# Attention kernel in one slot loop: the output projection as pairs of 64-row matmuls in two banks, and one maxima task moved by two groups

## The chip, the cores and the metric

The kernel runs on one core of one Trainium2 chip. The metric is the device time of one execution in microseconds. TensorE (PE) multiplies matrices into PSUM; ScalarE (ACT), VectorE (DVE) and GpSimd (POOL) do the rest, the first two from PSUM too; SyncE's queue (SP) issues most DMAs.

## What is computed

Two attention blocks over the same 2048 rows of 512 numbers, with 32 heads of 16, are mixed by a gate. All is in float32.

```python
def _A_ref(x, wq, wk, wv, wo, beta):     # 4 segments of 512 rows
    logits = jnp.einsum("bhqd,bhkd->bhqk", qs, ks) * scale + mask     # causal in the segment
    p = _softmax(logits, axis=-1)
    a_dot = jnp.einsum("bhqk,bhkd->bhqd", p, vs)
    a_mem = num / den                    # what the segments before left in M and z
    o = g * a_mem + (1.0 - g) * a_dot
    return o @ wo

def _B_ref(x, wqkv, wo):                 # all 2048 rows, no mask
    p = _softmax(jnp.einsum("bhqd,bhkd->bhqk", q, k) * (Dh ** -0.5), axis=-1)
    return (p @ v) @ wo

g = _sigmoid((x * gate_w).sum(-1, keepdims=True))
return g * _A_ref(...) + (1 - g) * _B_ref(...)
```

The weights of A are so large that its softmax needs exact row maxima. Products that must be exact are made from two halves of each number, a high and a low one, with three of the four terms (TERMS).

## The kernel before

After a first part (projections, memory of A) comes a loop of 32 **slots** `k`. A slot handles one unit of A and one of B; a unit is four heads by 512 queries. It has 37 **groups** `n`: 32 of B, then 5 of A. The program is written out in order and nothing reorders it: each engine works through its instructions as the Python code emits them.

In a group of B, TensorE does three things:

- the **score pair** (`t_group`, line 537): two matmuls with 64 rows of contraction, one on rows 0 to 63 and one on rows 64 to 127 of the array, into two banks of PSUM. ScalarE takes the exponential of each bank into `raw` (line 543);
- the **maxima pair** (`s_b`, line 474), a task for the next slot's unit: two 64-row matmuls into the two banks of a *score pair* buffer `sbk`; VectorE takes the maximum of both banks in one instruction (line 476). In groups 0 to 31 there is one such task, put between the two matmuls of the score pair (`mid`);
- the **products** with the values (`pv`, line 559) of an earlier group, into `pvb`.

PSUM has eight banks: `tb0`, `tb1` and `mb` for scores and anything else (`misc()` and the score pairs take the one used longest ago), `pvb`, and two buffers `sbk0` and `sbk1` of two banks each, which the maxima tasks use in turn (`rot("s", SBK)`). A matmul into a bank waits until the last reader of it is done.

In slots 9 to 30, group 1 also holds a call of the **output projection** for 128 rows of the segment before (`out_mm`, line 625): twelve matmuls with all 128 rows of contraction into one `misc()` bank. A call with `a == 0` does A's half, and ScalarE copies the bank to `yo` (line 629); the next slot's, with `a == 1`, does B's, VectorE adds the bank to `yo` (line 632), and SyncE's queue stores it. The operands `oh` and `ol` are made at the end of every second slot (`out_split`, line 618 on ScalarE and 619 on GpSimd). In group 0 the products of the slot before are finished and VectorE copies them out (`fin_copy`, line 566); SyncE's queue stores that copy and later loads parts of it back (`fin_load`, 576 and 578), and VectorE works on these from group 13 on (`fin_rec`, line 583).

Slot 0 has four groups (0, 2, 4, 6) with an own job of the first part (`fill`) and a second maxima task; both tasks stand between the two matmuls of the score pair there.

Of the kernel before, what the change touches and what calls it, by code (L numbers as in the profile page):

```python
# [7 lines left out]
FT = mybir.dt.float32  # L8
# [3 lines left out]
AF = mybir.ActivationFunctionType  # L12
OP = mybir.AluOpType
# [7 lines left out]
DM = 512  # L21
C = 512
NC4 = SEQ // C
NT = SEQ // 128
# [10 lines left out]
def gated_mix_kernel(ctx, tc, xt, wq, wk, wv, wo, beta, wqkv, wob, gate_w, out):  # L35
    nc = tc.nc
    outr = out.rearrange("b s d -> (b s) d")
# [47 lines left out]
    SBK = [PS.tile([128, 2, C], FT, name=f"sbk{i}") for i in range(2)]  # L85
    lru = []

    def bank(allowed):
        b = min(allowed, key=lambda a: max([n for n, x in enumerate(lru) if x is a], default=-1))
        lru[:] = [x for x in lru if x is not b] + [b]  # L90
        return b
# [3 lines left out]
    def misc():  # L95
        return bank(mode["misc"])
# [12 lines left out]
    def rot(key, lst):  # L109
        i = cnt.get(key, 0)  # L110
        cnt[key] = i + 1
        return lst[i % len(lst)]
# [165 lines left out]
    TERMS = ((0, 0), (0, 1), (1, 0))  # L278
# [127 lines left out]
    def load_q(u):  # L406
        kd, qd, c = UN[u]
        load_qk(q_of(u), kd, 0, qd, c)

    def load_ka(u):  # L410
        kd, qd, c = UN[u]
        load_qk(KA[u % 2], kd, 1, qd, c)

    def load_kb(k, c=None):
        dst = KB[k % 3] if c is None else KB[k % 3][:, :, c * C:(c + 1) * C]
        load_qk(dst, "B", 1, k % 8, c)
# [6 lines left out]
    def load_vb(g):  # L423
        v_src(VB[g % 2], "B", g % 4, None)

    def load_va(u):
        kd, qd, c = UN[u]
        v_src(VA[(u // 2) % 2], "A", qd // 2, c)
# [89 lines left out]
    AT = {}  # L518
# [102 lines left out]
    def out_mm(c, t, a):  # L621
# [8 lines left out]
        else:  # L630
            tt = 4 * c + t
            nc.vector.tensor_tensor(AT["yo"], b, AT["yo"], op=OP.add)
            nc.sync.dma_start(outr[tt * 128:(tt + 1) * 128, :], AT["yo"])

    def tail_ops(t):
        s = KB[2 * (t // 2)][:, t % 2]
        return [s[:, 1024 * n:1024 * n + 1024].rearrange("p (g a t) -> p g a t", g=4, a=2) for n in range(2)]
# [29 lines left out]
    def todo(fn, *a):  # L667
        return lambda: fn(*a)
# [90 lines left out]
    for blk in range(16):  # L759
        g, c = divmod(blk, 4)  # L760
# [8 lines left out]
        n = blk + 1 + (c == 2)  # L769
# [92 lines left out]
    def pvs(k, n):  # L862

        ua, ub = k, 32 + k
        if n == 0:
            if k:
                pv(ua - 1, 2)
                fin_copy(ua - 1)
        elif k == 31 and n < 2 * NT:
            if n % 2 and n > 1:  # L870
                pv(ub, n // 2 - 1)
        elif 2 <= n < 2 * NT + 2:
            pv(ub, n // 2 - 1, n % 2 * 256, n % 2 * 256 + 256)
            if n == 2 * NT + 1:
                fin_copy(ub)
        elif n > 2 * NT + 1:
            m = n - 2 * NT - 2
            if m < 2:
                pv(ua, 0, 256 * m, 256 * m + 256)
            else:  # L880
                pv(ua, 1)
                pv(ua, 3)

    def extras(k):

        pre, post = {}, {}
        if not k:
            for n in range(4):
                pre[2 * n] = [fill[n - 4]]
        post[2 * S_LAST + 4] = [todo(m_rows, k + 1)]  # L890
        for n, at in [(k - 9, 1)] + [(23, 2 * OMI)] * (k == 31):
            if n >= 0:
                pre[at] = [todo(out_mm, n // 8, n // 2 % 4, n % 2)]
        return pre, post

    def beside(k, it):
# [26 lines left out]


    ex = [extras(k) for k in range(32)]
    plan = {}

# [4 lines left out]
    for k in range(31):  # L932
# [5 lines left out]
        for n, t in enumerate(ST_A):  # L938
            plan.setdefault((k, 2 * NT + n - (n > 2)), []).append(todo(s_a, k + 1, *t))

    for k in range(32):
        ua, ub = k, 32 + k
        banks = T3 + [b[:, 0] for b in SBK] * (k == 31)
        for n in range(NG):
            it = n // 2 if n < NG - 1 else NT + 2
            mid = plan.pop((k, n)) if n < 2 * NT and (k, n) in plan else []
            t_group(*(ub, n) if n < 2 * NT else (ua, n - 2 * NT), banks, mid)
            for f in plan.get((k, n), []) + ex[k][0].get(n, []):
                f()
            pvs(k, n)  # L950
            for f in ex[k][1].get(n, []):
                f()
            if n % 2 == 0 and n < NG - 1:
                continue
            beside(k, it)
            if it == S_LAST:
                m_chain(k + 1)
            if it == 4 and not k:
                late()
            if it == 4 and not k:  # L960
                load_q(ub + 2)
                for c in range(NC4):
                    load_kb(2, c)
            if it == NT and k < 29:
                load_q(ub + 3)
                load_kb(k + 3)
            if it == 6 and k < 31:
                load_q(ua + 1)
                load_ka(ua + 1)
                if (ua + 1) % 2 == 0:  # L970
                    load_va(ua + 1)
            if it == 9:
                if k % 2 == 0 and k < 30:
                    load_vb(k // 2 + 1)
                if 1 <= k <= 4:
                    load_wo(k - 1)
# [55 lines left out]
```

## Time and profile before

| what | us |
|---|---|
| median of the runs | 1946.82 |
| fastest run | 1943.4 |
| the profiled execution | 1946.74 |
| its span | 1945.0 |
| TensorE busy in it | 1922.5 |
| VectorE busy | 1622.1 |
| ScalarE busy | 1434.8 |
| GpSimd busy | 298.4 |

A matmul's bar in the profile contains its weight load and its way through the array, so bars overlap and busy time says little; what counts is the distance from start to start. In the rows, `PEld` is the weight loads, a tile name like `tb<-qb,xh` is what is written and what is read, and `x4` is four instructions of one kind merged. TensorE's clock was granted in full in the whole span.

### The profile page before, as it was taken

The numbers are of one execution on the slowest core, as the hardware profiler recorded it, in microseconds if no ns is written. First come the engines' busy times: TensorE is split into PE (matmuls) and PEld (weight loads), VectorE is DVE, ScalarE is ACT, GpSimd is POOL, SyncE is SP. The second block draws the span as 40 slices with busy tenths as digits, with TensorE's granted clock in tenths as the row PEclk, the third lists the DMA queues.
The fourth block names the chain that finished last, engine by engine and source line by source line (L and its number), as shares of the span: only waits on it lengthen the run. The fifth ranks groups of instructions, "written<-read, shape, count | busy, mean of one in ns | idle before, by whom it ended". The sixth has DMA issues, their size and how long they took to land.

```text
span 1945.0 us, 43560 instructions
## 1 busy us (share of the span) xinstructions
PE 1922.5 (99%) x17485; PEld 931.0 (48%) x17485; DVE 1622.1 (83%) x1726; ACT 1434.8 (74%) x2699; POOL 298.4 (15%) x593
## 2 busy tenths in 40 slices
PE   7999999999999999999999999999999999999999
PEld 5887777444344444444444444444444444444445
DVE  6135766899999999999999999999999999999942
ACT  4233333688888888888888888888888888888884
POOL 5200000011111111111111111111111111111022
PEclk9999999999999999999999999999999999999999
DMA  7666656745444444443445454544444443434111
GB/s 217 163 207 185 196 193 173 176 96 116 98 117 88 105 87 105 87 116 87 116 87 114 87 115 87 116 88 108 94 97 107 96 105 87 104 87 110 50 48 58
DMA packets 163790, 222.49 MB, mean 114 GB/s; under 512 B 39916, under 2 KB 90556, under 8 KB 157828
## 3 DMA queue, kind: packets, MB, share of 16 engines
q1 hardware_dynamic: 159284, 211.41, 44.1%
q0 software_dynamic: 3248, 8.03, 2.3%
q8 instruction: 138, 2.26, 0.5%
q14 instruction: 64, 0.52, 0.1%
q10 hardware_dynamic: 1056, 0.26, 0.1%
HBM read 147.95 MB, written 68.16 MB: 111 GB/s over the span
## 4 chain that ended last, share of the span: by engine, by line
PE 96%; DVE 2%; DMA 1%; SPq 1%; issue 0%; ACT 0%; DVEq 0%; ACTq 0%
PE pvb L559 33%; PE tb L537 18%; PE sbk L474 12%; PE mb L537 9%; PE tb L304 5%; PE sbk L452 3%; PE tb L625 2%; PE mb L304 2%; PE sbk L287 1%; PE tb L287 1%; PE mb L625 1%; PE pvb L304 1%; PE sbk L456 1%; PE mb L287 1%; PE pvb L287 1%; PE tb L652 1%
## 5 line engine op out<-in xcount | busy, mean ns | idle before, releaser
L476 DVE TENSOR_REDUCE mxb<-sbk 128x2 f32<-128x1024 f32 x1024 | 1225.8, 1223 | 61.0 <-PE tb L537 30.6
L543 ACT ACTIVATE raw<-tb 128x512 f32<-128x512 f32 x1555 | 887.6, 598 | 148.2 <-PE tb L537 103.6
L559 PE MATMUL pvb<-raw,vb 128*17 128x256 f32 (+1 forms) x8072 | 639.9, 388 | 0.0
L543 ACT ACTIVATE raw<-mb 128x512 f32<-128x512 f32 x782 | 467.6, 598 | 72.3 <-PE mb L537 45.7
L474 PE MATMUL sbk<-xh,qb 64*128 64x512 f32 x1344 | 477.6, 444 | 3.5 <-DVE mxb L476 2.1
L537 PE MATMUL tb<-qb,xh 64*128 64x512 f32 x872 | 353.3, 443 | 0.0
L559 PEld LDWEIGHTS pvb<-raw,vb 128*17 128x17 f32 x8072 | 135.0, 95 | 341.3 <-issue 335.9
L474 PE MATMUL sbk<-kb,qb 64*128 64x512 f32 x704 | 240.9, 444 | 0.0
L537 PEld LDWEIGHTS tb<-qb,xh 64*128 64x128 f32 x872 | 146.4, 184 | 176.6 <-issue 90.1
L537 PE MATMUL mb<-qb,xh 64*128 64x512 f32 x445 | 199.0, 447 | 0.0
L474 PEld LDWEIGHTS sbk<-xh,qb 64*128 64x128 f32 x1344 | 190.6, 184 | 8.7 <-DVE mxb L476 6.3
L537 PE MATMUL tb<-qb,kb 64*128 64x512 f32 x470 | 191.0, 446 | 0.9 <-DVE st L314 0.9
L546 POOL TENSOR_SCALAR_AFFINE_SELECT raw<-raw 128x256 f32<-128x256 f32 (+1 forms) x320 | 115.6, 361 | 357.7 <-ACT raw L543 349.9
L460 DVE TENSOR_REDUCE mx<-sbk 128x2 f32<-128x768 f32 (+1 forms) x128 | 136.7, 1090 | 23.7 <-PE sbk L456 20.9
L537 PEld LDWEIGHTS mb<-qb,xh 64*128 64x128 f32 x445 | 82.0, 184 | 94.9 <-issue 50.6
L537 PEld LDWEIGHTS tb<-qb,kb 64*128 64x128 f32 x470 | 79.2, 184 | 99.0 <-issue 53.1
L599 POOL TENSOR_TENSOR o<-o,d 128x512 f32<-128x512 f32 x31 | 39.7, 1280 | 477.7 <-DMA d<-rd 388.5
L537 PE MATMUL mb<-qb,kb 64*128 64x512 f32 x234 | 104.1, 445 | 0.0
L474 PEld LDWEIGHTS sbk<-kb,qb 64*128 64x128 f32 x704 | 96.1, 184 | 5.2 <-issue 3.4
L559 PE MATMUL pvb<-raw,va 128*17 128x256 f32 (+2 forms) x1280 | 94.7, 384 | 0.8 <-ACT pvs L568 0.8
L452 PE MATMUL sbk<-ka,qa 64*128 64x256 f32 (+3 forms) x512 | 88.0, 358 | 1.1
L311 ACT ACTIVATE st<-tb 128x512 fp32r<-128x512 f32 x33 | 19.8, 599 | 81.1 <-DVE phi L310 46.8
(288 smaller groups left out, 1864.3 us busy)
## 6 DMA issues: line engine op xcount, KB each, us to landing
xh<-dB SPq DMA_DIRECT2D x38, 512.0 KB
vb<-vdB SPq DMA_DIRECT2D x16, 1088.0 KB
dB<-st SPq DMA_DIRECT2D x64, 256.0 KB
dA<-st SPq DMA_DIRECT2D x64, 256.0 KB
pd<-pvs SPq DMA_DIRECT2D x64, 256.0 KB
kb<-dB SPq DMA_DIRECT2D x22, 512.0 KB
xh<-dB SPq DMA_DIRECT2D x38, 256.0 KB
qb<-dB SPq DMA_DIRECT2D x64, 128.0 KB
```

Of the source, the lines that this page charges most:

```text
L287: nc.tensor.matmul(b, lhs, WV[wi][:, k, :], start=n == 0, stop=n == 11)
L304: nc.tensor.matmul(b, WS[ws][w][wi][:, k, :], (XH, XL)[xi][c][:, k, :], start=n == 0, stop=n == 11)
L452: nc.tensor.matmul(b[:, j, c0:c0 + n], q_of(u)[r, p, i * 128:(i + 1) * 128], k_of(u, p)[r, :n], start=True, stop=False)
L460: nc.vector.tensor_reduce(m[:, :, p, i], b[:, :, :n], axis=AX.X, op=OP.max)
L474: nc.tensor.matmul(b[:, j], q_of(u)[r, p, i * 128:(i + 1) * 128], k_of(u, p)[r, kc * C:(kc + 1) * C], start=True, stop=True)
L476: nc.vector.tensor_reduce(MXB[u][:, :, p, i, kc], b, axis=AX.X, op=OP.max)
L537: nc.tensor.matmul(bs[j][:, c0:c0 + w], k_of(u, h // 2)[r, 128 * it:128 * it + 128], q_of(u)[r, h // 2, q0:], start=True, stop=True)
L543: nc.scalar.activation(pt, bs[j], AF.Exp, scale=SCALE)
L546: nc.gpsimd.affine_select(out=m, in_=m, pattern=[[1, 128]] if n < 2 else [[0, 2], [1, 128]], compare_op=OP.is_ge, fill=0.0, base=0, channe ...
L559: nc.tensor.matmul(PVB[32 * h:32 * h + E + 1, q0 + lo:q0 + hi], vt[:, it, 4 * q + h, :], pt[:, lo:hi], start=it == 0 and lo == 0, stop=it ...
L599: nc.gpsimd.tensor_tensor(o, o, d, op=OP.mult)
L625: nc.tensor.matmul(b, (AT["oh"], AT["ol"])[oi][:, g, a], (AT["wh"], AT["wl"])[wi][:, g, a], start=n == 0, stop=n == 11)
```

## The change

`out_rows` takes the place of `out_mm` in slots 9 to 30. It cuts the contraction of 128 rows into two of 64, rows 0 to 63 (`j == 0`) and 64 to 127 (`j == 1`). The first sums up in a `misc()` bank, the second in the first bank of an `sbk` buffer, whose turn comes with it. So a call has 24 matmuls in place of 12, and two banks to take out of PSUM. With `a == 0` ScalarE copies the one to `yo` and VectorE the other to `yp`; with `a == 1` ScalarE copies the one to `yq`, VectorE adds the other to `yp`, and GpSimd makes two additions into `yo`, which SyncE's queue then stores.

In slots 9 to 30 the maxima task of group 2 is moved to group 0, where it takes the place between the score matmuls, and group 0's own task comes behind them. In group 1 the task is no longer between the score matmuls; it stands behind the projection. Group 2 has none. In slot 0, the second task of a group that has two stands behind the second score matmul and ahead of the own job.

```diff
@@ -631,6 +631,27 @@
             tt = 4 * c + t
             nc.vector.tensor_tensor(AT["yo"], b, AT["yo"], op=OP.add)
             nc.sync.dma_start(outr[tt * 128:(tt + 1) * 128, :], AT["yo"])
+
+    def out_rows(c, t, a):
+        b = [misc(), rot("s", SBK)[:, 0]]
+        for n, (oi, wi, g) in enumerate([(oi, wi, g) for oi, wi in TERMS for g in range(4)]):
+            for j in range(2):
+                r = slice(64 * j, 64 * j + 64)
+                nc.tensor.matmul(b[j], (AT["oh"], AT["ol"])[oi][r, g, a], (AT["wh"], AT["wl"])[wi][r, g, a],
+                                 start=n == 0, stop=n == 11)
+        if a == 0:
+            AT["y"] = [AT["L"].tile([128, DM], FT, name=n) for n in ("yo", "yp")]
+            nc.scalar.activation(AT["y"][0], b[0], AF.Copy)
+            nc.vector.tensor_copy(AT["y"][1], b[1])
+        else:
+            tt = 4 * c + t
+            y0, y1 = AT["y"]
+            y2 = AT["L"].tile([128, DM], FT, name="yq")
+            nc.scalar.activation(y2, b[0], AF.Copy)
+            nc.vector.tensor_tensor(y1, b[1], y1, op=OP.add)
+            nc.gpsimd.tensor_tensor(y0, y0, y2, op=OP.add)
+            nc.gpsimd.tensor_tensor(y0, y0, y1, op=OP.add)
+            nc.sync.dma_start(outr[tt * 128:(tt + 1) * 128, :], y0)
 
     def tail_ops(t):
         s = KB[2 * (t // 2)][:, t % 2]
@@ -890,7 +911,7 @@
         post[2 * S_LAST + 4] = [todo(m_rows, k + 1)]
         for n, at in [(k - 9, 1)] + [(23, 2 * OMI)] * (k == 31):
             if n >= 0:
-                pre[at] = [todo(out_mm, n // 8, n // 2 % 4, n % 2)]
+                pre[at] = [todo(out_rows if k < 31 else out_mm, n // 8, n // 2 % 4, n % 2)]
         return pre, post
 
     def beside(k, it):
@@ -938,14 +959,17 @@
         for n, t in enumerate(ST_A):
             plan.setdefault((k, 2 * NT + n - (n > 2)), []).append(todo(s_a, k + 1, *t))
 
+    for k in range(9, 31):
+        plan[k, 0] += plan.pop((k, 2))
     for k in range(32):
         ua, ub = k, 32 + k
         banks = T3 + [b[:, 0] for b in SBK] * (k == 31)
         for n in range(NG):
             it = n // 2 if n < NG - 1 else NT + 2
-            mid = plan.pop((k, n)) if n < 2 * NT and (k, n) in plan else []
+            mid = [plan[k, n].pop()] if n < 2 * NT and (k, n) in plan and (k < 9 or n != 1) else []
             t_group(*(ub, n) if n < 2 * NT else (ua, n - 2 * NT), banks, mid)
-            for f in plan.get((k, n), []) + ex[k][0].get(n, []):
+            own, tasks = ex[k][0].get(n, []), plan.get((k, n), [])
+            for f in own + tasks if k else tasks + own:
                 f()
             pvs(k, n)
             for f in ex[k][1].get(n, []):
```

What this makes of the order, in slot 10 (a call with `a == 1`). TensorE, groups 0 and 1, before: line 537 is the score pair, 474 the maxima pair, 559 the products, 625 the projection. What a row waits for stands in brackets.

```order
L537 MATMUL tb1_111<-qb0_68,xh0_87 128x512 [waits DMAHW1_49,DMAHW0_49]
L474 MATMUL sbk0_114<-xh1_88,qb1_69 128x512 [waits DVE_49]
L474 MATMUL sbk0_114<-xh1_88,qb1_69 128x512
L537 MATMUL tb0_110<-qb0_68,xh0_87 128x512 [waits Activation_49]
L559 MATMUL pvb_112<-raw8_86,va0_76 17x256 [waits Pool_49] x2
L559 MATMUL pvb_112<-raw8_86,va0_76 17x256 x2
L537 MATMUL mb_113<-qb0_68,xh0_87 128x512
L474 MATMUL sbk1_115<-xh1_88,qb1_69 128x512 [waits DVE_49]
L474 MATMUL sbk1_115<-xh1_88,qb1_69 128x512
L537 MATMUL tb1_111<-qb0_68,xh0_87 128x512 [waits Activation_49]
L625 MATMUL tb0_110<-wh_2776,oh_2780 128x512 [waits Activation_49]
L625 MATMUL tb0_110<-wh_2776,oh_2780 128x512 x3
```

TensorE, the same place after (line 640 is the new projection):

```order
L537 MATMUL tb1_111<-qb0_68,xh0_87 128x512 [waits DMAHW1_49,DMAHW0_49]
L474 MATMUL sbk1_115<-xh1_88,qb1_69 128x512 [waits DVE_49]
L474 MATMUL sbk1_115<-xh1_88,qb1_69 128x512
L537 MATMUL tb0_110<-qb0_68,xh0_87 128x512 [waits Activation_49]
L474 MATMUL sbk0_114<-xh1_88,qb1_69 128x512 [waits DVE_49]
L474 MATMUL sbk0_114<-xh1_88,qb1_69 128x512
L559 MATMUL pvb_112<-raw8_86,va0_76 17x256 [waits Pool_49] x2
L559 MATMUL pvb_112<-raw8_86,va0_76 17x256 x2
L537 MATMUL mb_113<-qb0_68,xh0_87 128x512
L537 MATMUL tb1_111<-qb0_68,xh0_87 128x512 [waits Activation_49]
L640 MATMUL tb0_110<-wh_2776,oh_2780 128x512 [waits Activation_49]
L640 MATMUL sbk1_115<-wh_2776,oh_2780 128x512 [waits DVE_49]
```

Group 0 now has two maxima tasks, into `sbk1` and `sbk0`, and group 1 none ahead of the projection; the projection's second bank is `sbk1`, the one that group 0's first task filled, with a wait for VectorE.

TensorE behind the projection, group 2 and the start of group 3, before:

```order
L625 MATMUL tb0_110<-wl_2777,oh_2780 128x512 x4
L625 MATMUL tb0_110<-wh_2776,ol_2781 128x512 x4
L537 MATMUL mb_113<-qb0_68,xh0_87 128x512 [waits Activation_49]
L474 MATMUL sbk0_114<-xh1_88,qb1_69 128x512 [waits DVE_49]
L474 MATMUL sbk0_114<-xh1_88,qb1_69 128x512
L537 MATMUL tb1_111<-qb0_68,xh0_87 128x512 [waits Activation_49]
L559 MATMUL pvb_112<-raw8_86,vb1_2773 17x256 [waits DVE_49]
```

And after, from the projection's last matmul on:

```order
L640 MATMUL tb0_110<-wh_2776,ol_2781 128x512
L640 MATMUL sbk1_115<-wh_2776,ol_2781 128x512
L474 MATMUL sbk0_114<-xh1_88,qb1_69 128x512 [waits DVE_49]
L474 MATMUL sbk0_114<-xh1_88,qb1_69 128x512
L537 MATMUL mb_113<-qb0_68,xh0_87 128x512 [waits Activation_49]
L537 MATMUL tb1_111<-qb0_68,xh0_87 128x512 [waits Activation_49]
L559 MATMUL pvb_112<-raw8_86,vb1_2773 17x256 [waits DVE_49]
L559 MATMUL pvb_112<-raw8_86,vb1_2773 17x256 x3
```

The maxima task of group 1 follows the projection at once, then the score pair of group 2, undivided, and the products.

VectorE at the same place, before: the last maximum of A's groups (line 462), group 0's maximum, the copy of the old products and group 1's maximum stand ahead of the projection's addition (line 632).

```order
L462 TENSOR_REDUCE mx_7803<-sbk1_115 128x4 [waits PE_49]
L476 TENSOR_REDUCE mxb_7649<-sbk0_114 128x2 [waits PE_49]
L566 COPY pvs_7938<-pvb_112 128x512 [waits DMAHW1_49,DMAHW5_49,PE_49,Activation_49]
L476 TENSOR_REDUCE mxb_7649<-sbk1_115 128x2 [waits PE_49]
L632 TENSOR_TENSOR yo_7427<-tb0_110,yo_7427 128x512 [waits PE_49]
L476 TENSOR_REDUCE mxb_7649<-sbk0_114 128x2 [waits PE_49]
```

VectorE after (line 651 is the addition from `sbk1`):

```order
L462 TENSOR_REDUCE mx_7817<-sbk0_114 128x4 [waits PE_49]
L476 TENSOR_REDUCE mxb_7663<-sbk1_115 128x2 [waits PE_49]
L476 TENSOR_REDUCE mxb_7663<-sbk0_114 128x2 [waits PE_49]
L566 COPY pvs_7955<-pvb_112 128x512 [waits DMAHW1_49,DMAHW5_49,PE_49,Activation_49]
L651 TENSOR_TENSOR yp_7440<-sbk1_115,yp_7440 128x512 [waits PE_49]
L476 TENSOR_REDUCE mxb_7663<-sbk0_114 128x2 [waits PE_49]
```

Two maxima of group 0 now stand ahead of the copy, and group 1's maximum stands behind the projection's addition.

## The prediction

> **What bounds the kernel now.** I read the page first: busy times, then the chain that ended last.
>
> ```profile
> span 1945.0 us, 43560 instructions
> PE 1922.5 (99%) x17485; PEld 931.0 (48%) x17485; DVE 1622.1 (83%) x1726; ACT 1434.8 (74%) x2699; POOL 298.4 (15%) x593
> PE 96%; DVE 2%; DMA 1%; SPq 1%; issue 0%; ACT 0%; DVEq 0%; ACTq 0%
> ```
>
> TensorE is 96% of the chain, so a gain must shorten what TensorE does or waits for. The profiled execution took 1946.74 us for this span (1.74 outside it), and the median of the runs is 1946.82, so the sum below stands for both. Next the chain of waits (start, length, what): the first two and the last of the output projections that it lists among its longest pieces, twenty in the 22 slots that the change touches, all of 2.95 to 2.98.
>
> ```profile
> 786.17 2.96 PE tb L625 x12
> 835.74 2.96 PE tb L625 x12
> ...
> 1777.56 2.96 PE mb L625 x12
> ```
>
> The distance from one to the next is 49.57 us, a slot. What such a place consists of, the timeline of TensorE shows; this is slot 14, groups 0 to 3 (start, length, operation).
>
> ```profile
> 1032.02 0.50 PE L537 MATMUL tb<-qb,xh 64*128 64x512 f32 x1
> 1032.03 0.73 PE L474 MATMUL sbk<-kb,qb 64*128 64x512 f32 x2
> 1032.36 0.39 PE L537 MATMUL mb<-qb,xh 64*128 64x512 f32 x1
> 1032.69 0.63 PE L559 MATMUL pvb<-raw,va 128*17 128x256 f32 x8
> 1033.24 0.50 PE L537 MATMUL tb<-qb,xh 64*128 64x512 f32 x1
> ...
> 1033.91 1.19 PE L625 MATMUL mb<-wh,oh 128*128 128x512 f32 x4
> 1034.94 1.09 PE L625 MATMUL mb<-wl,oh 128*128 128x512 f32 x4
> 1035.87 1.07 PE L625 MATMUL mb<-wh,ol 128*128 128x512 f32 x4
> 1036.87 0.50 PE L537 MATMUL tb<-qb,xh 64*128 64x512 f32 x1
> ...
> 1037.53 0.63 PE L559 MATMUL pvb<-raw,vb 128*17 128x256 f32 x8
> 1038.08 0.50 PE L537 MATMUL mb<-qb,xh 64*128 64x512 f32 x1
> ```
>
> Two facts are to be read from the starts. Two 64-row matmuls on the two halves of the array start 0.01 us apart (1032.02 and 1032.03) and run beside each other. And every stretch of one kind costs a fixed part besides its matmuls: four projections in the middle take 1035.87 - 1034.94 = 0.93, or 0.23 each, but all twelve 2.96, which is 12 x 0.23 + 0.20. A group's two pairs take 1032.69 - 1032.02 = 0.67, again 2 x 0.23 + 0.20. Three pairs in one stretch stand in slot 0, and take 363.77 - 362.88 = 0.89, which is 3 x 0.23 + 0.20.
>
> ```profile
> 362.88 0.49 PE L537 MATMUL tb<-qb,kb 64*128 64x512 f32 x1
> 362.88 0.95 PE L474 MATMUL sbk<-xh,qb 64*128 64x512 f32 x4
> ...
> 363.77 0.63 PE L559 MATMUL pvb<-raw,vb 128*17 128x256 f32 x8
> ```
>
> About half of the 0.20 is the first weight load, which nothing covers: in group 0 the second pair's load starts 0.11 after the first's.
>
> ```profile
> 1032.02 0.18 PEld L537 LDWEIGHTS tb<-qb,xh 64*128 64x128 f32 x1 [0.21 <-issue]
> ...
> 1032.13 0.19 PEld L537 LDWEIGHTS mb<-qb,xh 64*128 64x128 f32 x1
> ```
>
> **The projection itself.** Twelve full matmuls become 24 half ones, twelve pairs. At 0.23 a pair they take what they took. What goes is the change of kind around them: before, groups 0 to 2 hold four stretches (two pairs, two pairs, twelve projections, two pairs), 4 x 0.20 + 18 x 0.23 = 4.94. After, they hold two: three pairs, then the score pair of group 1, the twelve pairs, the maxima pair and the score pair of group 2: 2 x 0.20 + 18 x 0.23 = 4.54. That is 0.40 a call, if nothing waits.
>
> **The wait that comes with it.** The second bank is half of a score pair, and the order shows that it is the half just filled by the moved maxima task. VectorE's rows of the same place:
>
> ```profile
> 1032.79 1.23 DVE L476 TENSOR_REDUCE mxb<-sbk 128x2 f32<-128x1024 f32 x1 [0.95 <-PE mb L537]
> 1033.93 0.68 DVE L566 COPY pvs<-pvb 128x512 f32<-128x512 f32 x1
> ...
> 1036.97 0.69 DVE L632 TENSOR_TENSOR yo<-mb,yo 128x512 f32<-128x512 f32 x1 [1.23 <-PE mb L625]
> 1037.63 8.53 DVE L476 TENSOR_REDUCE mxb<-sbk 128x2 f32<-128x1024 f32 x7
> ```
>
> The first is the maximum of group 0, the copy is that of the old products, the addition at 1036.97 is the projection's, and the seven maxima after it are those of groups 2 to 8. I count from the start of group 0. Its first maximum starts at 0.77 and ends at 1.99. How long TensorE takes to go on after such an end is seen where a group in slot 13 waits for one: VectorE's maximum began at 1003.24, ends 1.22 later at 1004.46, and the held maxima matmul begins at 1004.51, so 0.05.
>
> ```profile
> 1003.24 2.35 DVE L476 TENSOR_REDUCE mxb<-sbk 128x2 f32<-128x1024 f32 x2
> 1004.36 0.50 PE L537 MATMUL tb<-qb,xh 64*128 64x512 f32 x1
> 1004.51 0.58 PE L474 MATMUL sbk<-xh,qb 64*128 64x512 f32 x2
> 1004.85 0.39 PE L537 MATMUL tb<-qb,xh 64*128 64x512 f32 x1
> ```
>
> So the projection's second half may load weights at 2.04 and run from 2.15. Without a wait: group 0 takes 0.89, its products 0.56 (1033.24 - 1032.69, rounded up), so group 1 begins at 1.45, and the projection would run from 1.45 + 0.11 + 0.23 = 1.79. The wait costs 0.36. From 2.15 follow 13 steps of 0.231 (eleven more pairs, the maxima pair, the score pair), to 5.15, and 0.33 from the last pair to the products (1032.36 to 1032.69): they start at 5.48. Before, they start at 1037.53 - 1032.02 = 5.51. What is left of 0.40 is 0.03 a call, 0.7 us in 22 calls. The half that doesn't wait runs one pair ahead and meets the other at the maxima pair, whose waiting half stands first, so that lead is worth nothing. Bounds: a gain of 0.39 if the wait costs nothing, a loss of 0.1 if the release or the restart takes 0.1 longer than in the one row.
>
> The Trainium skill, "TensorEngine Tiling (Array Packing)", section "Gotcha 1: PSUM Pressure", speaks against this change: row tiling raises the pressure on PSUM, as the row tiles must write to different banks. It gives no time; the trace above gives the price of the bank that has to be borrowed.
>
> **After the projection.** VectorE gets a 0.68 copy in the 11 calls that had none; in the other 11 its addition of 0.69 stays. It has room: in a slot of 49.5 us it is busy for 46.35.
>
> ```profile
> 1033.00:1082.50 49.50, 49.46 (x508) 20.82 (x504) 46.35 (x46) 41.31 (x78) 8.37 (x17) 1.00 0.49 114
> ```
>
> (The columns are TensorE, its weight loads, VectorE, ScalarE, GpSimd, clock, DMA.) And when behind, it catches up:
>
> ```profile
> 1052.80 3.48 DVE L476 TENSOR_REDUCE mxb<-sbk 128x2 f32<-128x1024 f32 x3
> ```
>
> Three maxima in 3.48, the last of 1.22, are one per 1.13, against a group of 1.22 (1036.87 to 1038.08, with rounding). The last pair runs from 2.15 + 11 x 0.231 = 4.69 and ends 0.39 later, at 5.08; the copy starts at 5.11 and ends at 5.80, and group 3, at 5.48 + 0.55 = 6.03, wants that buffer: 0.18 to spare with the 0.05. Group 1's maximum starts 0.66 after the copy (1036.97 to 1037.63), ends at 6.99; group 4 wants its buffer at 7.25: 0.21 to spare. Cost nothing; if both margins failed, some 0.2 a call.
>
> ScalarE's second copy (11 calls) costs a place of 0.49 in its row, at an end where it has been idle for 2 us:
>
> ```profile
> 987.41 0.60 ACT L629 ACTIVATE yo<-tb 128x512 f32<-128x512 f32 x1 [2.04 <-PE tb L625]
> 987.90 0.59 ACT L543 ACTIVATE raw<-mb 128x512 f32<-128x512 f32 x1
> ```
>
> The maxima pair stands between projection and scores and gives it 0.23 + 0.23 of cover; uncovered it is part of the 0.2 above.
>
> GpSimd's two additions, 1.28 each by its group of the same shape, and the output's DMA behind them; then rows of SyncE's queue and of VectorE:
>
> ```profile
> L599 POOL TENSOR_TENSOR o<-o,d 128x512 f32<-128x512 f32 x31 | 39.7, 1280 | 477.7 <-DMA d<-rd 388.5
> ...
> 1034.64 0.34 SPq L570 DMA_DIRECT2D pd<-pvs  x1
> ...
> 1045.57 0.53 SPq L576 DMA_DIRECT2D o<-pd  x1
> ...
> 1052.37 0.24 DVE L583 RECIPROCAL rec<-rec 128x16 f32<-128x16 f32 x1
> ```
>
> The store now holds SyncE's queue until about 5.1 + 0.6 + 2.6 = 8.3, or 1040.3 here; the next entry leaves at 1045.57, so nothing is behind it. The copy of the old products comes one maximum later (1.1 us), so the load at 1045.57 may go at 1046.7; its reader is at 1052.37. Zero; uncovered, at most 1.1 in a slot.
>
> **Slot 0.** Where a group has two maxima tasks, its second score matmul no longer stands behind the second task's wait. In the chain that matmul stands with 0.23 and 0.15 at two such groups, between the late task and the next job; the group at 362.88 above has no wait.
>
> ```profile
> 352.92 0.23 PE tb L537
> ...
> 359.26 0.15 PE mb L537
> ```
>
> Four groups of slot 0 are of that kind. I take 0.5 for the slot, between 0 and 0.9.
>
> Sum: 1946.74 - 0.7 - 0.5 = 1945.5.
>
> **The rivals.** *The wait doesn't count* (15%): VectorE gives the bank back early, or TensorE gets past it. Then 22 x 0.39 + 0.5 = 9.1 us go: 1937.6. For it stands that each step of 0.20 is in the rows; against it that the held instruction stands first in an in-order queue and the maximum's 1.22 is one instruction.
>
> *VectorE's hand-over* (20%), the one that ends slower: the copy after the projection holds the borrowed bank and delays group 1's maximum, so groups 3 and 4 wait. It decides once the margins of 0.18 and 0.21 are gone, that is when projection end to release takes 0.2 more; each call then loses 0.2 to 0.3, 22 x 0.25 = 5.5: 1951. Against it: VectorE recovers 0.09 a group, and the delay in slot 13 cost only 0.15 (0.49 from its first to its last score matmul, where 1032.02 to 1032.36 is 0.34).
>
> *Loads that don't hide* (4%): in a long run of half-array pairs each load stands open, 0.11 a pair: 22 x 12 x 0.11 = 29, 1974.6. The three pairs in 0.89 speak against it. The Trainium skill, "TensorE: Matmul & The Clock Gate", section "Part 3: Packing small matmuls", lets a weight load overlap a running matmul only if the row group differs, which would make this the likely case. By that rule the full projections, all on the same rows, would be 0.23 + 0.11 = 0.34 apart; the trace has 0.23, so the measurement decides.
>
> *The halves don't overlap* (2%): 24 steps of 0.23 instead of 12, 2.76 a call, 61 us: about 2006. The starts 0.01 apart speak against it.
>
> **How the numbers follow.** 59% stay with the sum, within 3 us. The range runs from 1937, where the first rival ends, to 1952, past the second; it leaves out the last two and the edges, some 1 in 10 by these cases, as bounds from single rows are soft. Changes under 2% (39 us) are what a measurement of this kernel can hardly tell from none; only the last rival goes beyond: faster 1%, within 96%, slower 3%.
>
> **What would show it.** The new projection's weight load should wait some 0.5 us (1.56 to 2.04) for VectorE's maximum, in all 22 slots; from its first to the next products 24 + 2 + 2 matmuls should show 0.23 a pair; group 3 should begin about 6.03 after group 0, and a slot remain 49.5. I am wrong if that wait is absent, if groups 3 to 5 show waits for VectorE, or if the slot shrinks by 0.3 or more.

## The result, and the profile after

| kernel | median, us | ratio to before (95 % interval) | one slot, us |
|---|---|---|---|
| before, run beside it | 1946.02 | | 49.571 |
| after | 1943.10 | 0.9988 (0.9983 to 0.9994) | 49.529 |

The medians are over all executions; the ratios leave out two slow ones, one of before (2188.65) and one of e6_longer_wait (3425.64, at a granted clock of 0.543), and aren't the quotients of these medians.

The changed kernel takes 1.2 to 3.3 us less (the interval times 1946), which is under 2% and so no change by the bound of the prediction. The forecast was 1945.5, with a range of 1937 to 1952. The kernel before, at 1946.02, lies in that range too, so the total alone tests little; the rows below test the mechanism. The page of the kernel after, its span, its busy times and the shares of its chain:

```profile
span 1942.3 us, 44163 instructions
PE 1919.8 (99%) x17749; PEld 941.6 (48%) x17749; DVE 1624.6 (84%) x1737; ACT 1440.5 (74%) x2710; POOL 326.9 (17%) x615
PE 94%; DVE 2%; DMA 1%; SPq 1%; issue 1%; ACT 0%; DVEq 0%
```

The bound is the same: TensorE is 94% of the chain. TensorE has 264 matmuls more (17749 - 17485), twelve in each of 22 calls, and isn't busier for it.

**A slot.** Line 507 makes a transpose once in a slot, always in the same form, and so marks the slots. These rows of TensorE's timeline are those of slot 8 and slot 29; between them lie 21 slots with a call each. Before:

```profile
767.50 0.39 PE L507 MATMUL tb<-ident,m 128*32 128x128 f32 x4
...
1808.49 0.39 PE L507 MATMUL tb<-ident,m 128*32 128x128 f32 x4
```

After:

```profile
765.97 0.39 PE L507 MATMUL tb<-ident,m 128*32 128x128 f32 x4
...
1806.08 0.39 PE L507 MATMUL tb<-ident,m 128*32 128x128 f32 x4
```

So a slot took (1808.49 - 767.50) / 21 = 49.571 and now takes (1806.08 - 765.97) / 21 = 1040.11 / 21 = 49.529: 0.042 less, 0.9 us in 22 slots.

**Inside a slot.** TensorE's timeline after, slot 14 again, from group 0 (1030.28) to group 3 (1036.28). The rows left out are further rows of the same stretches.

```profile
1030.28 0.50 PE L537 MATMUL tb<-qb,xh 64*128 64x512 f32 x1
...
1031.17 0.63 PE L559 MATMUL pvb<-raw,va 128*17 128x256 f32 x8
1031.72 0.50 PE L537 MATMUL tb<-qb,xh 64*128 64x512 f32 x2
1032.06 0.39 PE L640 MATMUL mb<-wh,oh 64*128 64x512 f32 x1
...
1033.35 0.39 PE L640 MATMUL sbk<-wl,oh 64*128 64x512 f32 x1
...
1034.94 0.39 PE L640 MATMUL sbk<-wh,ol 64*128 64x512 f32 x1
1034.98 0.58 PE L474 MATMUL sbk<-kb,qb 64*128 64x512 f32 x2
...
1035.73 0.63 PE L559 MATMUL pvb<-raw,vb 128*17 128x256 f32 x8
1036.28 0.50 PE L537 MATMUL mb<-qb,xh 64*128 64x512 f32 x1
```

The weight loads at the start of the projection, same kernel and slot. In brackets stand the idle time before a row and what ended it.

```profile
1031.95 0.18 PEld L640 LDWEIGHTS mb<-wh,oh 64*128 64x128 f32 x1
...
1032.33 0.18 PEld L640 LDWEIGHTS sbk<-wh,oh 64*128 64x128 f32 x1 [0.19 <-DVE mxb L476]
```

And VectorE's timeline there: the two maxima of group 0, the copy of the old products, the projection's addition, and the maxima that follow.

```profile
1031.05 2.36 DVE L476 TENSOR_REDUCE mxb<-sbk 128x2 f32<-128x1024 f32 x2 [0.94 <-PE sbk L474]
1033.32 0.68 DVE L566 COPY pvs<-pvb 128x512 f32<-128x512 f32 x1
...
1035.37 0.69 DVE L651 TENSOR_TENSOR yp<-sbk,yp 128x512 f32<-128x512 f32 x1 [1.37 <-PE sbk L474]
1035.98 4.74 DVE L476 TENSOR_REDUCE mxb<-sbk 128x2 f32<-128x1024 f32 x4
```

Counted from the start of group 0, at 1030.28:

| event | predicted | after |
|---|---|---|
| first half of the projection runs | 1.79 | 1.78 |
| second half's weight load | 2.04 | 2.05 |
| one pair | 0.231 | 0.227 (1.59 / 7, from 1033.35 to 1034.94) |
| VectorE's addition starts | 5.11 | 5.09 |
| products of group 2 | 5.48 | 5.45 |
| next maximum | 5.77 | 5.70 |
| group 3 | 6.03 | 6.00 |

Group 3's score matmuls start at 1036.28 and 1036.62 and its maxima pair at 1036.29, the 0.34 of a group without a wait, so VectorE gave the buffer back in time.

**The waits.** The view of waits of the kernel after, its three groups of weight loads at line 640 (us in all, times, longest one):

```profile
PEld sbk L640 <- DVE mxb L476: 2.1, 11, 0.2
...
PEld tb L640 <- ACT raw L543: 1.8, 7, 0.3
...
PEld mb L640 <- ACT raw L543: 1.0, 4, 0.3
```

Only half of the 22 calls show VectorE, with 0.19 each. The other eleven are the calls with `a == 0`. There the end of a segment's `out_split` (a row of 1.06 on ScalarE ahead of group 0's exponentials) makes the exponentials late, and the projection's *first* bank is held back by ScalarE, to about 1.88. The second half still waits for VectorE until 2.04, but no longer long enough to be a row of its own: idle time counts from the end of the load before. In slot 14, too, the second half's load is 0.38 behind the first's (1032.33 - 1031.95), and only 0.19 of it is idle in this view, since the load before ended at 1031.95 + 0.18 = 1032.13.

In slot 14 ScalarE is close behind as well. Its exponential of the projection's first bank:

```profile
1031.31 0.59 ACT L543 ACTIVATE raw<-mb 128x512 f32<-128x512 f32 x1
```

It ends at 1031.90, and the first half's load goes at 1031.95, which is 1.67 after group 0. That costs nothing here, since the matmul (1.78) stands behind the score pair anyhow.

**Slot 0.** The two profiled spans differ by 1945.0 - 1942.3 = 2.7, but 0.9 of it lies in the 22 slots. A part of the rest isn't the change. These are windows of 3.41 us in slot 0 (window; length; then busy time of TensorE, its weight loads, VectorE, ScalarE, GpSimd; granted clock; DMA share; GB/s). Before:

```profile
345.48:348.89 3.41, 3.41 (x9) 2.63 (x9) 1.34 (x2) 0.49 (x1) 0.00 (x0) 0.50 0.73 241
```

After:

```profile
345.48:348.89 3.41, 3.41 (x23) 1.97 (x21) 1.48 (x2) 0.66 (x2) 1.28 (x2) 1.00 0.75 225
```

In the chain of before the job that stands there is this step (start, length):

```profile
345.34 4.56 PE mb L304 x12
```

And in the chain of after:

```profile
344.84 2.99 PE mb L304 x12
```

The profiled execution of before ran these matmuls at half the clock for 3.41 us, which cost 4.56 - 2.99 = 1.57. (The sentence ahead of the prediction, that the clock was granted in full in the whole span, misses this stretch.) It isn't a property of the one kernel or the other, as the second experiment shows. A second stretch at about half the clock, which the sentence misses too, lies between 52 and 59 us in both profiles (0.52 before, 0.53 after), and so makes no difference between them. So the time of the change is better read from the slots and from the ratio of the runs than from two spans.

### The profile page after: what moved, and what is told of

Its sections match the earlier page's. It is cut to its first block, busy times and chain, and to the rows that moved or that the text cites. A ratio compares the mean times of both kernels' runs of the same rounds, so it can differ in the third digit from the quotient of the medians.

```text
span 1942.3 us, 44163 instructions
## 1 busy us (share of the span) xinstructions
PE 1919.8 (99%) x17749; PEld 941.6 (48%) x17749; DVE 1624.6 (84%) x1737; ACT 1440.5 (74%) x2710; POOL 326.9 (17%) x615
## 4 chain that ended last, share of the span: by engine, by line
PE 94%; DVE 2%; DMA 1%; SPq 1%; issue 1%; ACT 0%; DVEq 0%
PE pvb L559 33%; PE tb L537 17%; PE sbk L474 12%; PE mb L537 9%; PE tb L304 4%; PE sbk L452 3%; PE sbk L640 2%; PE mb L304 2%; PE sbk L287 1%; PE tb L287 1%; PE pvb L304 1%; PE sbk L456 1%; PE mb L287 1%; PE pvb L287 1%; DVE mxb L476 1%; PE tb L640 1%
## 5 line engine op out<-in xcount | busy, mean ns | idle before, releaser
L474 PE MATMUL sbk<-xh,qb 64*128 64x512 f32 x1344 | 467.8, 442 | 3.6 <-DVE mxb L476 2.2
L474 PE MATMUL sbk<-kb,qb 64*128 64x512 f32 x704 | 236.2, 442 | 0.2 <-DVE mxb L476 0.2
```

Source lines behind the costliest of these rows:

```text
L474: nc.tensor.matmul(b[:, j], q_of(u)[r, p, i * 128:(i + 1) * 128], k_of(u, p)[r, kc * C:(kc + 1) * C], start=True, stop=True)
```

## The experiments

The theory, W, is that of the prediction: the projection loses its fixed parts (0.40 a call), and the wait of its second half for VectorE's first maximum takes nearly all of it back. Against it stand that the gain is in slot 0 or comes from moving tasks, that the wait is hidden, and that VectorE's hand-over behind the projection is what costs. A *slot* is the distance between the rows of line 507, as above. The kernel before had a median of 1944.87 beside e1, e2, e4 and e5 and of 1946.20 beside e3, e6, e7 and e8, so go by the ratios and the slots, not by the medians of different rows.

| label | what it is | median, us | ratio to before (95 % interval) | one slot, us |
|---|---|---|---|---|
| after | all parts | 1943.10 | 0.9988 (0.9983 to 0.9994) | 49.529 |
| e1_slot0_only | slot 0's order alone | 1945.32 | 1.0004 (0.9994 to 1.0014) | 49.576 |
| e2_tasks_moved_only | all but the new projection | 1944.82 | 0.9998 (0.9987 to 1.0010) | 49.563 |
| e6_longer_wait | a bank filled later | 1970.44 | 1.0125 (1.0109 to 1.0142) | 50.678 |
| e3_task_not_moved | all but the moved task | 1962.44 | 1.0086 (1.0069 to 1.0104) | 50.390 |
| e8_pair_banks_only | both banks from one pair | 1954.17 | 1.0051 (1.0035 to 1.0068) | 50.052 |
| e4_task_in_group36 | the task one group earlier still | 1945.24 | 1.0013 (1.0001 to 1.0026) | 49.653 |
| e5_task_first_in_group0 | the task first in group 0 | 1939.73 | 0.9973 (0.9964 to 0.9982) | 49.388 |
| e7_first_and_pair_banks | e5 and e8 together | 1950.37 | 1.0028 (1.0017 to 1.0040) | 49.840 |

### One part alone: slot 0's order

The kernel after, with the old projection and the tasks where they were:

```diff
-                pre[at] = [todo(out_rows if k < 31 else out_mm, n // 8, n // 2 % 4, n % 2)]
+                pre[at] = [todo(out_mm, n // 8, n // 2 % 4, n % 2)]
...
-    for k in range(9, 31):
-        plan[k, 0] += plan.pop((k, 2))
...
-            mid = [plan[k, n].pop()] if n < 2 * NT and (k, n) in plan and (k < 9 or n != 1) else []
+            mid = [plan[k, n].pop()] if n < 2 * NT and (k, n) in plan else []
```

> The kernel before with slot 0's new order alone: the second maxima task behind the second score matmul; projection and task places as before. Theory W (the slots 9 to 30 keep only 0.04 a call, 0.9 us in all, because the wait for the borrowed bank eats 0.36 of 0.40): slot 0 gives the rest, three score matmuls of 0.23 taken out of the chain, 0.7 us, and 2.3 us in an execution in which the kernel before falls to half clock for 3.41 us there. So 1943.7 to 1945.4 with 1946.0 for before, and slots 9 to 30 at 49.57 us each as before. Rival N (the gain of the change lies in the new projection): no change here, 1946.0, and group 0 of slot 0 at its old length of 3.4 us.

The groups with two tasks are where the gain should be. TensorE's timeline before, from such a group's first score matmul to its products:

```profile
357.85 0.49 PE L537 MATMUL tb<-qb,kb 64*128 64x512 f32 x1
...
362.32 0.63 PE L559 MATMUL pvb<-raw,vb 128*17 128x256 f32 x8
```

The same group in this kernel:

```profile
354.00 0.50 PE L537 MATMUL tb<-qb,kb 64*128 64x512 f32 x1
...
358.25 0.63 PE L559 MATMUL pvb<-raw,vb 128*17 128x256 f32 x8
```

4.47 before, 4.25 here, and 4.25 after too: 0.22, one matmul that no longer stands behind a wait. Three groups of slot 0 gain that, 0.7 us in all; the fourth, group 0, takes as long as before, for no task waited there. The slots stay as before (49.576), as they must. The runs can't show 0.7: the interval reaches from 1.2 us less to 2.7 more.

### One part alone: the tasks moved, the old projection kept

```diff
-                pre[at] = [todo(out_rows if k < 31 else out_mm, n // 8, n // 2 % 4, n % 2)]
+                pre[at] = [todo(out_mm, n // 8, n // 2 % 4, n % 2)]
```

> The changed kernel with the old projection, twelve 128-row matmuls into one bank: the moved task, the task behind the projection and slot 0's order stay. Theory W: three stretches in groups 0 to 2 cost 0.89 (three pairs), 0.56 (products), 0.43 (score pair alone), 2.96, then 0.66 (two pairs), so the products of group 2 start 5.50 after group 0, as before (5.50) and 0.04 later than in the changed kernel; slots stay at 49.57; the time is that of slot 0's order alone, 1943.7 to 1945.4. Rival N (moving the tasks is itself the gain, by keeping VectorE fed in the projection): the products at 5.46 or less and the time of the changed kernel, 1943.1.

TensorE's timeline of this kernel in slot 15, group 0 and the products of group 2:

```profile
1081.07 0.50 PE L537 MATMUL mb<-qb,kb 64*128 64x512 f32 x1
...
1086.57 0.62 PE L559 MATMUL pvb<-raw,vb 128*17 128x256 f32 x8
```

5.50 from the one to the other, where before had 5.49 in the same slot, and a slot of 49.563 against 49.571. Moving the tasks earns next to nothing by itself; of the 0.042 a slot of the kernel after, 0.034 comes with the new projection. This kernel's profile also had half a clock, 0.52, in the very window of slot 0 where before had 0.50 and after 1.00, and that of the first experiment had 0.54 from 378.00 to 385.50. This kernel's row of the window, with the columns as above:

```profile
345.48:348.89 3.41, 3.41 (x9) 2.67 (x9) 1.59 (x2) 0.00 (x0) 0.00 (x0) 0.52 0.71 240
```

So the stretch comes and goes from one profile to the next, with the new order of slot 0 as with the old one.

### Does the wait count? A bank that VectorE gives back later

One more turn of the score pair buffers gives the projection the other one, which the *second* maximum of group 0 holds. Nothing else changes, and the wait is longer by a maximum.

```diff
     def out_rows(c, t, a):
+        rot("s", SBK)
         b = [misc(), rot("s", SBK)[:, 0]]
```

> The changed kernel with the projection borrowing the other pair, the one that group 0's second maxima task fills. Theory W: its second half waits for the end of the second maximum (1.91 + 1.22 + 0.05 = 3.18) instead of the first (2.04); the products of group 2 start 1.14 later, at 6.60; 22 calls make 25 us: about 1968, ratio 1.0115. Rival N (TensorE would have waited for something else anyhow): less than half of that, under 12 us.

TensorE's timeline of this kernel, group 0 and the products of group 2 of slot 14:

```profile
1038.73 0.50 PE L537 MATMUL tb<-qb,xh 64*128 64x512 f32 x1
...
1045.32 0.63 PE L559 MATMUL pvb<-raw,vb 128*17 128x256 f32 x8
```

Its weight loads, the second half of the projection:

```profile
1041.90 0.18 PEld L641 LDWEIGHTS sbk<-wh,oh 64*128 64x128 f32 x1 [1.32 <-DVE mxb L476]
```

And its waits:

```profile
PEld sbk L641 <- DVE mxb L476: 26.8, 22, 1.3
```

The load goes at 3.17 (expected 3.18) in place of 2.05, and the products start at 6.59 (expected 6.60) in place of 5.45. A maximum's place of 1.12 more in the wait is 1.14 more in the products and 50.678 - 49.529 = 1.15 more in the slot. The wait stands on the path one to one, and is a row of its own in all 22 calls. The lead of the first half is worth nothing: it was 1.1 us longer here and bought nothing. That rules out the rival by which the wait doesn't count.

### Is the moved task needed? The projection without it

```diff
-    for k in range(9, 31):
-        plan[k, 0] += plan.pop((k, 2))
```

> The changed kernel without the moved task: the task of group 2 stays in group 2, the one of group 1 stays behind the projection, which now borrows the pair that A's last group used, free long before. Theory W, by the rows of the run with the task in the last group: the projection waits for ScalarE's exponential only (weight load at 1.67 after group 0), but group 2's task wants the borrowed bank back while VectorE still adds or copies it: projection's end at 4.7, VectorE done at 5.43, the task's weight load at 5.48 instead of 4.67. The products of group 2 then start at about 6.15 against 5.50 before: 0.65 a call, 14 us slower than before, ratio 1.007. Rival N (the place of the task is no matter): within 1.5 us of the changed kernel.

Here the projection takes a buffer that is long free, and doesn't wait for VectorE. But the next task but one, that of group 2, wants the same buffer right behind it, and stands until VectorE has taken the projection's half out. The waits of this kernel at line 474:

```profile
PEld sbk L474 <- DVE yp L645: 9.4, 11, 0.9
PEld sbk L474 <- DVE yp L651: 8.7, 11, 0.8
```

Its timeline of TensorE in slot 14, group 0, the maxima pair of group 2 that is held, and the products:

```profile
1033.99 0.49 PE L537 MATMUL tb<-qb,xh 64*128 64x512 f32 x1
...
1039.51 0.49 PE L474 MATMUL sbk<-kb,qb 64*128 64x512 f32 x2 [0.35 <-DVE yp L651]
1040.17 0.63 PE L559 MATMUL pvb<-raw,vb 128*17 128x256 f32 x8
```

6.18 to the products (expected 6.15) against 5.45, and 22 waits of 18.1 us. The interval of the ratio is 13 to 20 us slower; 14 had been expected, from the calls with an addition alone, and the others, in which VectorE copies (line 645), lose some 0.3 more. So the move buys time between the projection and the next use of its buffer, and is paid with the wait in front of it: without the move a slot is 0.82 longer than before (50.390 - 49.571), with it 0.04 shorter.

### The hand-over's margin: both banks from one pair

The projection takes both banks of one score pair buffer, and none of the `misc()` banks.

```diff
-        b = [misc(), rot("s", SBK)[:, 0]]
+        s = rot("s", SBK)
+        b = [s[:, 0], s[:, 1]]
```

> The changed kernel with both banks of the projection from the borrowed pair, the task order unchanged. Theory W: VectorE's release at 1.99 sets both halves; the half that ran ahead before now waits too, which is worth nothing; the products of group 2 stay at 5.46 and slots at 49.53, the time that of the changed kernel within 1 us. Rival (the lead of the first half or ScalarE's bank is worth something): slots differ by more than 0.05.

The load stays at 2.05 and the products at 5.45 to 5.50 in all calls, as W says. Here the first half waits too, so the wait is a row in all 22 calls, of 0.40 each:

```profile
PEld sbk L641 <- DVE mxb L476: 8.9, 22, 0.4
```

But the time, which was to stay within 1 us, is some 11 us longer (22 slots of 0.52). The loss is behind the products. ScalarE's timeline of this kernel at the end of the projection in slot 14:

```profile
1034.97 0.60 ACT L651 ACTIVATE yq<-sbk 128x512 f32<-128x512 f32 x1 [1.98 <-PE sbk L641]
```

VectorE's:

```profile
1035.60 0.69 DVE L652 TENSOR_TENSOR yp<-sbk,yp 128x512 f32<-128x512 f32 x1 [2.03 <-ACT yq L651]
```

And TensorE's, group 3 from its first score matmul to its products:

```profile
1035.88 0.49 PE L537 MATMUL mb<-qb,xh 64*128 64x512 f32 x1
...
1037.01 0.63 PE L559 MATMUL pvb<-raw,vb 128*17 128x256 f32 x8
```

Both readers now read the same buffer, and VectorE's read stands behind ScalarE's: it begins at 1035.60, where ScalarE's began at 1034.97 and took 0.60. VectorE is 0.63 later: its addition starts 1035.88 - 1035.60 = 0.28 ahead of group 3, in the kernel after 1036.28 - 1035.37 = 0.91 ahead. Group 3 takes 1.13 in place of 0.66 (two pairs and their fixed part), 0.47 more. 0.63 - 0.47 = 0.16 is the margin that was there, and the prediction had worked out 0.18 for it. In the calls with a copy group 3 takes 1.20, and a slot is 50.052 - 49.529 = 0.52 longer in the mean. So the second rival's mechanism is real, and it starts where the prediction put it; the change as made stays short of it.

### Take the wait away: the task in the group before

The moved task goes to the last group of the slot before (`plan[k - 1, 2 * NT + 4]`), so that the projection's buffer is given back earlier.

```diff
-        plan[k, 0] += plan.pop((k, 2))
+        plan[k - 1, 2 * NT + 4] += plan.pop((k, 2))
```

> The changed kernel with the maxima task of group 2 moved one group further ahead, to the end of the last group of the slot before: the borrowed bank is then free at about 1.0 us after group 0's start, ahead of the projection (1.56). The same matmuls in the same number. Theory W: no wait of the projection for VectorE; products of group 2 start 4.89 after group 0 instead of 5.46, the last group gets 0.23 longer, so 0.34 a call, 7.5 us less than the changed kernel: 1935.6. Rival N (the wait is not what holds the projection; VectorE or ScalarE behind it would): the wait goes from the projection and comes back in groups 3 to 5 as waits for VectorE; the time stays at 1943, within 1.5.

TensorE's timeline of this kernel: the last group of slot 13 in the first three rows, then group 0 of slot 14 and the products of its group 2.

```profile
1026.34 0.38 PE L537 MATMUL mb<-qa,ka 64*128 64x256 f32 x1
...
1027.18 0.49 PE L474 MATMUL sbk<-kb,qb 64*128 64x512 f32 x2
1027.60 1.06 PE L559 MATMUL pvb<-raw,va 128*17 128x384 f32 x16
1028.59 0.50 PE L537 MATMUL tb<-qb,xh 64*128 64x512 f32 x1
...
1033.70 0.63 PE L559 MATMUL pvb<-raw,vb 128*17 128x256 f32 x8
```

VectorE's timeline ahead of it, the last two maxima of A:

```profile
1025.90 2.03 DVE L462 TENSOR_REDUCE mx<-sbk 128x4 f32<-128x1024 f32 x2 [0.23 <-PE sbk L456]
```

VectorE's wait is gone, and the products start at 5.11 instead of 5.45. But 4.89 had been expected, as group 0 has a pair less: now ScalarE's exponential, which ends at 1030.21, holds the projection's first bank (its load goes at 1030.26). And the task isn't cheap where it went. The last group takes 1027.60 - 1026.34 = 1.26, where it took 0.78 after, 0.48 more for a pair of 0.23: the task's buffer is held by a maximum of A, the first of the two in VectorE's row, which takes 1.23, and the weight load goes 0.05 behind its end. 0.48 - 0.34 = 0.14 a slot is lost, against 49.653 - 49.529 = 0.12 measured. So the expected gain of 0.34 a slot became a loss; that the wait is gone from the front is shown, that taking it away pays is not.

### Shorten the wait: the task first in group 0

The moved task comes ahead of group 0's score pair, so that VectorE's first maximum begins a pair earlier. Only the order of the instructions changes.

```diff
-            mid = [plan[k, n].pop()] if n < 2 * NT and (k, n) in plan and (k < 9 or n != 1) else []
+            if n == 0 and 9 <= k < 31:
+                plan[k, 0].pop()()
+            mid = [plan[k, n].pop()] if n < 2 * NT and (k, n) in plan and (k < 9 or n > 1) else []
```

> The changed kernel with the moved task at the very start of group 0, ahead of the score pair: its second matmul starts with its first, not 0.34 later. Theory W: VectorE's maximum starts 0.54 after group 0 instead of 0.77 and the borrowed bank is free 0.23 earlier; the projection's second half may load at 1.81, so the wait is 0.13 instead of 0.36, and the products of group 2 start at 5.24: 0.23 a call, 5.1 us less than the changed kernel: 1938. Rival N: no change against 1943.1, within 1.5, since what comes behind the projection sets the time.

TensorE's timeline of this kernel, the first pair of group 0 of slot 14 and the products of group 2:

```profile
1028.94 0.50 PE L474 MATMUL sbk<-kb,qb 64*128 64x512 f32 x2
...
1034.28 0.63 PE L559 MATMUL pvb<-raw,vb 128*17 128x256 f32 x8
```

Its weight loads, the first half of the projection:

```profile
1030.84 0.18 PEld L640 LDWEIGHTS mb<-wh,oh 64*128 64x128 f32 x1 [0.27 <-ACT raw L543]
```

This is the fastest of all, faster than before and than the change: 0.9973 of before, and a slot of 49.388, 0.14 less than after (0.23 had been expected). VectorE's maximum begins 0.23 earlier, but the products come only 0.11 earlier (5.34; 5.24 had been expected), for the score pair is now a pair later, ScalarE's exponential with it, and the projection's first bank waits for that until 1.90. From there the prediction's count holds again: 1.90 + 0.11 + 13 x 0.231 + 0.33 = 5.34. The slots account for (49.571 - 49.388) x 22 = 4.0 us and slot 0's order for 0.7; the interval of the ratio is 3.5 to 7.0 us less.

### Both at once

e5 with both banks from one pair, so that no bank of ScalarE's exponentials is wanted:

```diff
-        b = [misc(), rot("s", SBK)[:, 0]]
+        s = rot("s", SBK)
+        b = [s[:, 0], s[:, 1]]
```

> The run with the moved task at the start of group 0, and in addition both banks of the projection from the borrowed pair, none from the score banks. In that run the projection's first weight load stood 1.90 after group 0, 0.05 after ScalarE's exponential of the first bank ended (1.85); VectorE's maximum ended at 1.77. Theory W2 (ScalarE's release of the first bank is what that run waited for): the load now goes at 1.82, 0.09 a call earlier, slots of 49.30 instead of 49.39, 1.9 us less than that run. Rival (VectorE's release held it, or ScalarE's copies come in the way of group 3): slots stay at 49.39 or grow.

In slot 14 the products come 5.25 after the first pair of group 0, 0.09 earlier than in e5: ScalarE's bank was indeed the last thing they waited for. But the 0.46 that group 3 waits for VectorE is there again, and a slot is 49.840, where 49.30 had been expected. A bank that is free earlier isn't worth a reader that is free later.

## Why the prediction was right

**The size.** It was right in sign and size: 0.7 us were forecast for the 22 slots, and they gave 0.9; 0.5 for slot 0, and the three groups of its rows gave 0.7, which the runs of the first experiment can't confirm. Together 1.6, inside the 1.2 to 3.3 of the runs. The medians differ by 2.9; what of that goes beyond 1.6 isn't explained by any row, and the interval doesn't demand it.

**The fixed part of a stretch and 0.23 a pair.** Right. The two stretches have no other gaps, and the weight loads of half-array pairs hide: a pair is 0.227 in slot 14, against 0.231 forecast, which would make 0.05 over the 13 steps behind the wait; the products there start 0.03 earlier than the 5.48 forecast. Over all 22 calls they start at 5.44 to 5.48, 5.46 in the mean, where before has 5.47 to 5.52 and 5.50. So a call gained 0.04 where 0.03 had been forecast. (The list of the chain that the prediction shows first holds nineteen projections of these slots, not twenty; nothing hangs on it.)

**The wait.** Right as a cost: 2.05 for the load where 2.04 was forecast, and the experiment with the longer wait moves the products one to one. Three theories of why the change does little would all have given about 1945: that wait, no gain from the pairs, or a loss behind the projection. That it is the wait is shown by lengthening it (1.15 a slot lost) and by shortening it (0.14 a slot gained).

**What would show it.** This step was wrong as it was written: "some 0.5 us ... for VectorE's maximum, in all 22 slots". The view shows 0.19, in 11 of them. One reason is how idle time is counted, from the end of the load before: where both halves wait, with both banks from one pair, it shows 0.40 in all 22. The other is a fact that the prediction overlooked: ScalarE's exponential gives the *first* bank back at nearly the same time (the load goes 1.67 after the start of group 0 in the one kind of call and 1.88 in the other), and is next in line. The total didn't suffer, since the second half is still later. But it is why the two experiments that took VectorE's wait away got 0.34 and 0.11 a call at the products of group 2, where 0.56 (5.45 - 4.89) and 0.21 (5.45 - 5.24) had been expected.

**The hand-over.** The margin of 0.18 was right (0.16 by the pair of banks), group 3 starts at 6.00 (6.03), and groups 3 to 5 have no wait for VectorE. The rival of 1951 had a price of 0.25 a call; where the margin was really passed, by 0.47, it was 0.5.

**ScalarE's second copy, GpSimd's additions, the store, the later copy of the old products.** Nothing was expected and nothing is seen. That a slot is shorter by all that the front of it gained leaves no room for a cost elsewhere.

**Slot 0.** A matmul that no longer stands behind a wait is 0.22 a group, at three groups. The bigger difference between the two profiles there, 1.57, is the half clock of the execution of before, which the prediction had not seen and didn't need. At slot 8's row of line 507 the kernel after is only 767.50 - 765.97 = 1.53 ahead, less than 0.7 + 1.57; what of that is due to the transfers that slots 0 to 8 wait for, the two traces don't tell.

## What to carry to other kernels

Matmuls of different shapes in turn pay a fixed part at each change of kind, 0.20 us here, and giving the odd one the shape of its neighbours removed two of them; but when the new shape needs a bank more, ask of every bank who read it last and who wants it next, since each 0.1 us of that wait comes off the gain. Before a limiter is removed, look for the second one behind it: here ScalarE gave its bank back only 0.16 to 0.37 us ahead of VectorE (1.88 and 1.67 against 2.04), and took 0.22 of 0.56 and 0.10 of 0.21 of what the better orders should have earned. And with 0.4 us at stake, the order of two matmul pairs that cost nothing was worth more ((49.529 - 49.388) x 22 = 3.1 us) than the rewritten projection (0.9 us) on which it builds; what that order would give with the old projection was not tried.

## What the runs showed of the hardware that had not been expected

Stretches in which TensorE was granted half its clock, 3.41 us long or about twice that, appear in slot 0 in some profiles (before, the first and the second experiment), in that with the longer wait shortly ahead of it (0.50 from 322.12 to 328.95), and not in the others. The Trainium skill, "TensorE: Matmul & The Clock Gate", section "Part 1: The HAM clock gate", states a window of 3413 ns that isn't tied to the program; the 3.41 us of the trace agree with its length. Three of the four profiles named have the new order of slot 0, so it doesn't prevent such a stretch; whether it makes one rarer, so few profiles can't tell.

The granted clock also goes with most of the spread between executions: of the 22 of the kernel after, the three with a mean of 0.997 took 1944.3 to 1946.2, the eight with 0.999 took 1940.0 to 1942.2. So 0.002 of the clock goes with some 4 us, more than the whole change, and executions are best compared at one clock: at 0.998, fifteen of before have a median of 1944.78 and five of e5 beside them one of 1940.25, 4.5 less, where slots and slot 0 account for 4.7.

Two engines that read the two banks of one buffer did so one behind the other, with VectorE's row naming ScalarE's as what it waited for, where they read two separate tiles at once in the kernel after (ScalarE from 1035.18 for 0.60, VectorE from 1035.37 for 0.69). Whether the banks themselves would allow both reads at once isn't shown; the wait is one that the program contains.
